# Attention with a two-layer expert tail on one core: GpSimd's first key copies and multiplications in a fixed order, block maxima and value sums moved on VectorE, weight decoding one unit later

## The chip, the core and the metric

The kernel runs on one core of one Trainium2 chip. The metric is the device time of one launch in microseconds. TensorE is PE in the rows (its weight loads are PEld), VectorE is DVE, ScalarE is ACT, GpSimd is POOL and SyncE is SP; a q behind the name (SPq, DVEq) is the sequencer of that engine.

## The reference, cut to what matters

```python
# attention: q, k, v are (2, 8, 768, 64)
k_sum = k.reshape(B, H, nb, block, D).max(axis=3)      # blocks of 32 keys: their maxima
v_sum = v.reshape(B, H, nb, block, D).mean(axis=3)     # and the means of their values
scores_l = scale * q @ k.T                             # kept where |i - j| < 16
scores_s = scale * q @ k_sum.T + log(block)
a = softmax(concat(scores_l, scores_s))                # exp, row sum, divide
x = a @ concat(v, v_sum)                               # then (1536, 512) tokens
# first layer, d_ff 2048
h = x @ moe_w_in
y = (h * sigmoid(1.702 * h)) @ moe_w_out
# second layer, d_ff 1536
out = (sigmoid(y @ moe2_w_gate) * (y @ moe2_w_val)) @ moe2_w_out
```

## The kernel before, in words

The attention is cut into 24 units, `units[u] = (b, g, hp)`: two batches b, three groups g of four query blocks of 64, four pairs of heads hp. Units 0 to 11 are of the first batch, 12 to 23 of the second. A unit goes through these steps, each a function of its own:

- `w_copy`: the keys that the four query blocks see, and the block maxima beside them, are copied and scaled into a tile `kx`, in two instructions (L698 on ScalarE for units 0 and 1, L700 on GpSimd from unit 2). The block maxima `ks` are made once for each batch and pair of heads by `prep_k` (L686, VectorE), so the second instruction of a `kx` waits for them.
- `b_pe` (L720, L722, TensorE): the scores `ps_s`. `b_max` (L728, VectorE): the row maxima `nm`. `b_exp` (L736, ScalarE): four exponentials with row sums `sm`.
- `n_inv` (L743, L745, VectorE): reciprocal `rr` of the sums. `n_mul` (L750, GpSimd): `e` times `rr`.
- `c_pe` (L756), `c_copy` (L761): transposes `ps_p` and their copy `pt`. `d_pe` (L775): values, `ps_x`. `d_hi` (L793, ScalarE) and `d_lo` (L796, VectorE): the token tile in two parts, `xH` and `xL`.

Beside the units run the value sums (`sum_v`, L668, VectorE, from the transposed values `vt`; `sum_lay`, L677 and L680, which ends in the tile `vs`: `vs_112` for the first batch, `vs_113` for the second), the decoding of weights (`load`: VectorE L132, L150 and L155, ScalarE L142 and L153; a matrix piece arrives as `raw` and leaves as `w..H` and `w..L`), and the first four of the expert layers' steps (`filler`: `first`, whose products are `ps_h` at L487, with the sigmoid at L514 and the gating at L498, L506 and L507; `second`, whose products are `ps_o` at L487).

A loop over t from -1 runs the list `ORDER` of (step, lag) at each t, step on unit t minus lag. That is only the order in which the program is written. A scheduler decides the order in which each of TensorE, VectorE, ScalarE and GpSimd gets its instructions, from its own estimate of times; at the chip each engine then works strictly in that order. Three things bind the scheduler: `in_turn` makes VectorE's attention instructions follow one another as written while t is at most `ORDERED` (4); `behind(ins, ahead["kx"])` keeps GpSimd's key copies of units 2 to 7 behind the tile that it clears at the start; and SyncE, which issues the transfers, keeps the written order. SyncE's queue is therefore one line: `vwin<-vs` of the second batch (L647) must wait for `vs_113` (L680 on ScalarE), and behind it in the queue come the keys `k` of the last pair of heads (L623, needed by unit 15), the next weights and the last queries.

Of the kernel before, what the change touches and what calls it, by code (L numbers as in the profile page):

```python
# [14 lines left out]
ALU = mybir.AluOpType  # L15
AX = mybir.AxisListType
PSUM = bass.MemoryType.PSUM
P = 128
# [11 lines left out]
def attention_moe_moe2_kernel(ctx: ExitStack, tc: tile.TileContext, ins: dict, out: bass.AP):  # L30
    nc = tc.nc
# [4 lines left out]
    B, HP, _, S = vt.shape  # L36
    H, D = 2 * HP, 64
# [5 lines left out]
    W0 = 32  # L43
    M0 = W0 + HALO
    G = 4
# [7 lines left out]
    scale = 1.0 / float(D) ** 0.5  # L53
# [55 lines left out]
    turn, ahead = [], {}  # L109

    def behind(a, b):

        tc.add_manual_dep(
            a.ins, b.ins.name,
            mybir.DependencyInfo(mybir.DependencyClass.NoSync, mybir.DependencyReason.DATA), reason="order",
        )
# [100 lines left out]
    for layer, g, i in wanted:  # L217
        w = mats[layer][i]
        last = i == len(mats[layer]) - 1
        x = w.bitcast(U32)  # L220
# [288 lines left out]
    def first(layer, g, blk, batch=False):  # L509
        w = weights[layer, g, 0]  # L510

        def sigmoid(layer, ps):
            sg = sg_slots.tile([P, TB], F32, "sg")
            nc.scalar.activation(sg, ps, AF.Sigmoid, scale=1.702 if layer == 1 else 1.0)  # L514
            return sg

        def gated(f, ps, sg):
            gate_by((layer, g, blk, f), ps, sg)

        if batch:  # L520
            held = []
            for f in range(GF):
                held.append(project(w[0], w[1], f, blk, "ps_h"))
                yield
            held = [(ps, sigmoid(layer, ps)) for ps in held]
            yield
            for f, (ps, sg) in enumerate(held):
                gated(f, ps, sg)
            yield
            return  # L530
        for f in range(GF):
            ps = project(w[0], w[1], f, blk, "ps_h")
            gated(f, ps, sigmoid(layer, ps))
            yield
# [54 lines left out]
    def pull(n):  # L589
        for _ in range(n):  # L590
            next(coming, None)

    def need(*keys):
        for key in keys:
            tries = 0
            while key not in weights:
                pull(1)
                tries += 1
                assert tries < 100, (key, w_free, w_held)

    with tc.manual_schedule(engines={mybir.EngineType.SP}), ExitStack() as es:
# [10 lines left out]
        vwin = one.tile([P, 2 * G, H * D], F32, name="vwin")  # L612
# [4 lines left out]
        qbd, vsum, kraw, kmax, kx = {}, {}, {}, {}, {}  # L617
# [8 lines left out]
        def load_q(u, eng):  # L626

            b, g, hp = units[u]
            t = qp.tile([P, G, P], F32, tag="q", name=f"q{u}")
            eng.dma_start(out=t.rearrange("p i c -> p (i c)"), in_=q[b, g, hp])  # L630
            qbd[u] = t
# [32 lines left out]
        def sum_v(b, hp):  # L664
            if hp == 0:
                vpart[b] = vp.tile([P, HP, W0], F32, tag="vm", name=f"vm{b}")
                nc.vector.memset(vpart[b], 0.0)
            in_turn(nc.vector.tensor_reduce(  # L668
                out=vpart[b][:, hp, 0:NB], in_=vtl.pop((b, hp)).rearrange("p (n t) -> p n t", t=BLK),
                axis=AX.X, op=ALU.add,  # L670
            ))

        def sum_lay(b):
            r = vpart.pop(b)
            ps = ps_a.tile([W0, H * D], F32, tag="x", name="ps_v", bufs=2)
            for hp in range(HP):
                ins = nc.tensor.matmul(ps[:, hp * P:(hp + 1) * P], lhsT=r[:, hp], rhs=ident, start=True, stop=True)  # L677
                if b == 0:
                    behind(ins, live["last"])
            nc.scalar.activation(vsum[b][0:W0], ps, AF.Copy, scale=1.0 / BLK)  # L680

        def prep_k(b, hp):
            ks = kp.tile([P, W0], F32, tag="ks", name=f"ks{b}_{hp}")
            nc.vector.memset(ks, 0.0)
            own = kraw[b, hp][:, HALO:HALO + S].rearrange("p (n t) -> p n t", t=BLK)
            in_turn(nc.vector.tensor_reduce(out=ks[:, 0:NB], in_=own, axis=AX.X, op=ALU.max))  # L686
            kmax[b, hp] = ks

        def w_copy(u):

            b, g, hp = units[u]
            t = kxp.tile([P, G, P], F32, tag="kx", name=f"kx{u}")
            r = kraw[b, hp][:, g * G * QB:g * G * QB + P - W0]
            src = bass.AP(r.tensor, r.offset, [r.ap[0], [QB, G], [1, P - W0]])
            top = kmax[b, hp].unsqueeze(1).to_broadcast([P, G, W0])
            for to, x in ((t[:, :, W0:P], src), (t[:, :, 0:W0], top)):
                if u < 2:
                    nc.scalar.activation(to, x, AF.Copy, scale=scale)  # L698
                    continue
                ins = nc.gpsimd.tensor_scalar(out=to, in0=x, scalar1=scale, scalar2=None, op0=ALU.mult)  # L700
                if u < 2 * HP:
                    behind(ins, ahead["kx"])
            kx[u] = t

        live = {}
# [1 line left out]
        def in_turn(ins):  # L707

            if now[0] <= ORDERED:
                if turn:  # L710
                    behind(ins, turn[-1])
                turn.append(ins)

        now, ORDERED = [-1], 4

        def b_pe(u):
            b, g, hp = units[u]
# [29 lines left out]

        def n_mul(u):
            e, rr = live["e", u], live.pop(("rr", u))
            nc.gpsimd.tensor_tensor(out=e, in0=e, in1=rr.unsqueeze(2).to_broadcast([P, G, P]), op=ALU.mult)  # L750

        def c_pe(u):
            e = live.pop(("e", u))
# [41 lines left out]
        def d_lo(u):  # L795
# [4 lines left out]
        NU = len(units)  # L800
        LN, LC, LD = 1, 3, 3
        ORDER = [
            (w_copy, -1), (b_pe, 0), (b_max, 0), (n_inv, LN), (n_mul, LN),
            (c_pe, LC), (c_copy, LC), (d_pe, LD), (d_hi, LD), (b_exp, 0), (d_lo, LD),
        ]

# [3 lines left out]
        for _ in range(10):  # L810
# [31 lines left out]
            out=win, in_=win, pattern=[[0, NSLOT], [1, P - W0]], compare_op=ALU.is_gt, fill=NEG,  # L842
            base=0, channel_multiplier=-1,
        )
        ins = nc.gpsimd.affine_select(
            out=win, in_=win, pattern=[[0, NSLOT], [-1, P - W0]], compare_op=ALU.is_gt, fill=NEG,
            base=2 * HALO, channel_multiplier=1,
        )
        for x in (vwin[0:W0, 0:G, :], vsum[0]):
            zero = nc.gpsimd.memset(x, 0.0)  # L850
            behind(zero, ins)
            ins = zero
# [9 lines left out]
        def filler():  # L862
            for layer, g, blk in steps[:EARLY]:
                while (blk + 1) * 2 * HP - 1 + LD > now[0]:
                    yield
                need((1, g, 0))
                yield from first(layer, g, blk, batch=True)
                need((1, g, 1))
                yield from second(layer, g, blk, False, True)

        fill = filler()
        for t in range(-1, NU + LD):
            now[0] = t

            u = t + 2
            if t < 0:
                prep_k(0, 1)
            elif HP <= u < NU and units[u][1] == 0:
                prep_k(units[u][0], units[u][2])
            for part, lag in ORDER:  # L880
                late = lag == LD and part not in (c_pe, c_copy)
                if late and t == LD + 1:
                    part(0)
                if part is w_copy and 0 < t < HP - 1:
                    continue
                if 0 <= t - lag < NU and not (late and t == LD):
                    part(t - lag)
                if part is b_max:
                    if 0 < t < HP - 1:
                        prep_k(0, t + 1)  # L890
                        w_copy(t + 1)
                    if t in (0, 1, 3, 4):
                        sum_v(0, {0: 0, 1: 1, 3: 2, 4: 3}[t])
                    if t == 4:
                        sum_lay(0)
                        nc.vector.tensor_copy(
                            vwin[0:W0, G:2 * G, :], vsum[0][0:W0].unsqueeze(1).to_broadcast([W0, G, H * D])
                        )
            if 0 <= t < NU - QUERIES:
                load_q(t + QUERIES, nc.sync)  # L900
            if t == 0:
                load_v(0, 1)
                fetch()
            if t in (5, 8):
                fetch()
            if t in (7, 8, 9, 10):
                sum_load(1, t - 7)
            if t in (8, 9, 10, 11):
                sum_v(1, t - 8)
            if t == 11:  # L910
                sum_lay(1)

            if t % HP == HP - 1 and HP < t < NU - HP:
                c = t // HP + 1
                load_v(c // NG, c % NG)
                put_v(c // NG, c % NG)
            if 8 <= t < 8 + HP:
                load_k(1, t - 8)
            if t > ORDERED:
                pull(1 if t > 9 else 2)  # L920
            for _ in range(2 if t >= 8 else 1):
                next(fill, None)
# [151 lines left out]
```

## Time and profile before

| | us |
|---|---|
| median of 3 runs (lowest, highest) | 628.85 (627.6, 629.54) |
| the profiled execution, its time | 628.51 |
| its span, first to last instruction | 626.7 |
| TensorE busy in the span | 604.9 |
| VectorE, ScalarE, GpSimd busy | 466.3, 307.1, 213.3 |
| mean granted TensorE clock, as a share of full speed | 0.992 |

A row of a timeline gives the start and the duration of an instruction (or of a few alike, with their count), its line, what it writes and reads, and in brackets how long the engine was idle before it and who ended that. Times are from the start of the span. 1.81 us of the execution's time lie outside the span.

### The profile page before, as it was taken

To read this page: it belongs to the slowest core of one execution; us is meant where nothing else is said; L and a number is where in the kernel's file an instruction comes from. 1 tells how busy PE (TensorE), PEld (TensorE's weight loads), DVE (VectorE), ACT (ScalarE), POOL (GpSimd) and SP (SyncE) were. 2 spreads that over 40 slices of the span, in tenths; PEclk is the share of its full clock that TensorE was granted. 3 is DMA by queue.
4 is the path that set the end of the run, shared out by engine and by line. 5 is a ranking of instruction groups with operands and counts; after the bars stand their busy time and mean duration, and the time that the engine had idled before them with its cause. 6 is when DMAs were issued, how large, how long until landed. Compare 5 with 4: busy or idle time off the path is not lost.

```text
span 626.7 us, 8835 instructions
## 1 busy us (share of the span) xinstructions
PE 604.9 (97%) x3360; PEld 503.0 (80%) x3360; DVE 466.3 (74%) x685; ACT 307.1 (49%) x616; POOL 213.3 (34%) x166
## 2 busy tenths in 40 slices
PE   5889979999999999999999999999999999999997
PEld 3766767778887888888888888888888888898896
DVE  6589755469898779696769979766977777877434
ACT  4489655746443345343445557653434434344230
POOL 5967864314264423241332231120220121131030
PEclk9899989999999999999999999999999999999999
DMA  9996833014221123021202003420411221100014
GB/s 312 362 325 213 250 127 67 3 47 155 68 70 65 68 67 122 13 68 67 68 1 68 0 1 135 134 68 1 134 68 44 91 68 61 75 1 1 0 41 160
DMA packets 25017, 57.83 MB, mean 92 GB/s; under 512 B 1552, under 2 KB 1808, under 8 KB 24976
## 3 DMA queue, kind: packets, MB, share of 16 engines
q1 hardware_dynamic: 24400, 56.24, 27.1%
q10 hardware_dynamic: 576, 1.05, 0.4%
q8 instruction: 26, 0.43, 0.3%
q14 instruction: 15, 0.12, 0.1%
HBM read 53.08 MB, written 3.15 MB: 90 GB/s over the span
## 4 chain that ended last, share of the span: by engine, by line
PE 79%; DMA 6%; issue 5%; ACT 4%; POOL 3%; DVE 3%; SPq 0%; ACTq 0%; POOLq 0%; DVEq 0%
PE ps_o L487 32%; PE ps_y L191 15%; PE ps_x L191 10%; PE ps_v L191 10%; PE ps_h L487 5%; PE ps_h L191 3%; DMA q<-in_q 2%; POOL gl L507 2%; DMA vt<-in_vt 2%; PE ps_s L722 2%; DMA raw<-in_moe_w_out 1%; PE ps_x L775 1%; ACT e L736 1%; PE ps_p L756 1%; DMA k<-in_k 1%
## 5 line engine op out<-in xcount | busy, mean ns | idle before, releaser
L507 POOL TENSOR_TENSOR gl<-sg,gh 128x512 fp32r<-128x512 f32 x84 | 126.1, 1507 | 368.6 <-ACT gh L506 263.1
L570 DVE TENSOR_TENSOR acc<-ps_o,acc 128x512 f32<-128x512 f32 x143 | 95.9, 684 | 46.8 <-PE ps_o L487 46.6
L487 PE MATMUL ps_o<-gl,w_1H 128*128 128x512 f32 x192 | 75.5, 394 | 1.2 <-POOL gl L507 1.2
L487 PE MATMUL ps_o<-gh,w_1L 128*128 128x512 f32 x192 | 72.2, 397 | 3.3 <-DVE sg L498 2.7
L487 PE MATMUL ps_o<-gh,w_1H 128*128 128x512 f32 x192 | 74.9, 391 | 0.0
L506 ACT CAST gh<-sg 128x512 fp32r<-128x512 f32 x84 | 51.4, 619 | 47.0 <-DVE sg L498 37.6
L487 PE MATMUL ps_o<-w_2L,gh 128*128 128x512 f32 (+1 forms) x146 | 56.6, 388 | 0.0
L487 PE MATMUL ps_o<-w_2H,gh 128*128 128x512 f32 (+1 forms) x146 | 56.2, 386 | 0.0
L487 PE MATMUL ps_o<-w_2H,gl 128*128 128x512 f32 (+1 forms) x146 | 56.2, 389 | 0.1
L150 DVE SCALAR_TENSOR_TENSOR da<-da,db 128x1024 uint32<-128x1024 uint32 x34 | 45.7, 1344 | 5.7 <-ACT da L142 5.1
L142 ACT ACTIVATE da<-da 128x1024 f32<-128x1024 f32 x34 | 36.2, 1063 | 26.1 <-DVE da L132 24.3
L487 PEld LDWEIGHTS ps_o<-gh,w_1L 128*128 128x128 f32 x192 | 35.9, 188 | 12.4 <-DVE sg L498 3.2
L487 PEld LDWEIGHTS ps_o<-gl,w_1H 128*128 128x128 f32 x192 | 36.2, 189 | 9.4 <-POOL gl L507 2.4
L487 PEld LDWEIGHTS ps_o<-gh,w_1H 128*128 128x128 f32 x192 | 36.2, 189 | 7.4
L487 PE MATMUL ps_h<-xL,w_0H 128*128 128x512 f32 x96 | 37.8, 394 | 1.8 <-DVE xL L796 1.8
L487 PE MATMUL ps_h<-xH,w_0L 128*128 128x512 f32 x96 | 37.7, 403 | 0.0
L487 PE MATMUL ps_h<-xH,w_0H 128*128 128x512 f32 x96 | 37.4, 390 | 0.0
L736 ACT ACTIVATE e<-ps_s,nm 128x128 f32<-128x128 f32 x96 | 34.4, 385 | 4.7 <-DVE nm L728 2.9
L722 PEld LDWEIGHTS ps_s<-kx,q 128*128 128x128 f32 x192 | 26.6, 206 | 9.8 <-POOL kx L700 7.3
L750 POOL TENSOR_TENSOR e<-e,rr 128x512 f32<-128x512 f32 x24 | 27.4, 1145 | 19.0 <-DVE rr L745 13.7
L722 PE MATMUL ps_s<-kx,q 128*128 128x128 f32 x192 | 27.6, 291 | 4.8 <-DMA q<-in_q 3.1
L700 POOL TENSOR_SCALAR kx<-k 128x384 f32<-128x384 f32 x22 | 29.0, 1323 | 9.0 <-DMA k<-in_k 7.8
(245 smaller groups left out, 1507.1 us busy)
## 6 DMA issues: line engine op xcount, KB each, us to landing
raw<-in_moe_w_out SPq DMA_DIRECT2D x13, 1024.0 KB, 4.8
raw<-in_moe_w_in SPq DMA_DIRECT2D x8, 1024.0 KB, 6.9
raw<-in_moe_w_gate SPq DMA_DIRECT2D x6, 1024.0 KB, 5.2
raw<-in_moe_w_val SPq DMA_DIRECT2D x6, 1024.0 KB, 5.0
q<-in_q SPq DMA_DIRECT2D x20, 256.0 KB, 8.6
vwin<-in_v SPq DMA_DIRECT2D x6, 768.0 KB, 8.0
k<-in_k SPq DMA_DIRECT2D x8, 400.0 KB, 6.5
out<-acc SPq DMA_DIRECT2D x11, 256.0 KB, 2.0
```

The source lines that it names most:

```text
L142: ins = nc.scalar.activation(af, af, AF.Prelu, scale=REBIAS, alpha=-2.0 ** 32)
L150: nc.vector.scalar_tensor_tensor(out=a, in0=a, scalar=3, in1=b, op0=ALU.logical_shift_left, op1=ALU.bitwise_or)
L191: nc.tensor.matmul(ps, lhsT=a[x][:, kk, :], rhs=b[y][:, kk, :], start=start and i == 0, stop=i == n - 1, skip_group_check=True,)
L487: nc.tensor.matmul(ps, lhsT=a, rhs=b, start=i == 0, stop=i == n - 1)
L506: nc.scalar.copy(gh, sg)
L507: nc.gpsimd.tensor_tensor(out=gl, in0=sg, in1=gh, op=ALU.subtract)
L570: nc.vector.tensor_tensor(out=a[:, m, :], in0=ps, in1=a[:, m, :], op=ALU.add)
L700: ins = nc.gpsimd.tensor_scalar(out=to, in0=x, scalar1=scale, scalar2=None, op0=ALU.mult)
L722: ins = nc.tensor.matmul(ps[:, j, :], lhsT=t[:, j, :], rhs=kt[:, j, :], start=False, stop=j == G - 1)
L736: ahead["exp"] = nc.scalar.activation(e[:, j, :], s[:, j, :], AF.Exp, bias=nm[:, j:j + 1], accum_out=sm[:, j:j + 1])
L750: nc.gpsimd.tensor_tensor(out=e, in0=e, in1=rr.unsqueeze(2).to_broadcast([P, G, P]), op=ALU.mult)
L756: nc.tensor.transpose(ps[:, j, :], e[:, j, :], ident)
```

## The change

GpSimd's chain becomes explicit: a new helper `spread` puts each of its key copies and multiplications of units 0 to 7 behind the one written before it. The written order itself is changed: within one t the row maxima come first, `w_copy` moves behind `n_inv` and runs two units ahead in place of one, and a table `between` names what is written behind which step: the block maxima of unit 3 behind the reciprocal of unit 0 (t = 1), the value sums of pairs 2 and 3 at t = 3 instead of 3 and 4, `sum_lay(0)` behind the scores of unit 4. `ORDERED` goes from 4 to 5, which also lets the decoding of weights (`if t > ORDERED: pull(...)`) begin one unit later. No instruction is added or taken away.

```diff
+        def spread(ins, u):
+
+            if u < 2 * HP:
+                behind(ins, ahead["kx"])
+                ahead["kx"] = ins
...
-                ins = nc.gpsimd.tensor_scalar(out=to, in0=x, scalar1=scale, scalar2=None, op0=ALU.mult)
-                if u < 2 * HP:
-                    behind(ins, ahead["kx"])
+                spread(nc.gpsimd.tensor_scalar(out=to, in0=x, scalar1=scale, scalar2=None, op0=ALU.mult), u)
...
-        now, ORDERED = [-1], 4
+        now, ORDERED = [-1], 5
...
-            nc.gpsimd.tensor_tensor(out=e, in0=e, in1=rr.unsqueeze(2).to_broadcast([P, G, P]), op=ALU.mult)
+            spread(nc.gpsimd.tensor_tensor(out=e, in0=e, in1=rr.unsqueeze(2).to_broadcast([P, G, P]), op=ALU.mult), u)
...
-            (w_copy, -1), (b_pe, 0), (b_max, 0), (n_inv, LN), (n_mul, LN),
+            (b_pe, 0), (b_max, 0), (n_inv, LN), (w_copy, -2), (n_mul, LN),
...
+        between = {
+            (b_max, 0): [lambda: sum_v(0, 0)],
+            (b_max, 1): [lambda: prep_k(0, 2)],
+            (n_inv, 1): [lambda: prep_k(0, 3), lambda: w_copy(2)],
+            (b_max, 2): [lambda: sum_v(0, 1)],
+            (b_max, 3): [lambda: sum_v(0, 2), lambda: sum_v(0, 3)],
+            (b_pe, 4): [lambda: sum_lay(0)],
+            (b_max, 4): [means],
+        }
...
-                if part is b_max:
-                    if 0 < t < HP - 1:
-                        prep_k(0, t + 1)
-                        w_copy(t + 1)
-                    if t in (0, 1, 3, 4):
-                        sum_v(0, {0: 0, 1: 1, 3: 2, 4: 3}[t])
-                    if t == 4:
-                        sum_lay(0)
...
+                for then in between.get((part, t), ()):
+                    then()
```

Since the scheduler works from the written order, the instructions move on every engine up to the point where unit 20 or so is reached; behind it all five engines have the same order as before. Three places follow.

GpSimd at the start, before (the tiles `kx_239`, `kx_267`, `kx_283`, `kx_315` are those of units 2, 3, 4 and 5):

```order
L700 TENSOR_SCALAR kx_239<-ks_2_236 128x4x32
L700 TENSOR_SCALAR kx_267<-k_3_154 128x4x96
L700 TENSOR_SCALAR kx_283<-k_0_138 128x4x96
L700 TENSOR_SCALAR kx_283<-ks_0_194 128x4x32
L750 TENSOR_TENSOR e<-e,rr 128x512
L700 TENSOR_SCALAR kx_315<-k_1_142 128x4x96
L700 TENSOR_SCALAR kx_315<-ks_1_197 128x4x32
L700 TENSOR_SCALAR kx_267<-ks_3_264 128x4x32
L750 TENSOR_TENSOR e<-e,rr 128x512
```

The same place in the change (`kx_246`, `kx_249`, `kx_274`, `kx_300` are those of units 2, 3, 4 and 5):

```order
L706 TENSOR_SCALAR kx_246<-ks_2_236 128x4x32
L706 TENSOR_SCALAR kx_249<-k_3_154 128x4x96
L706 TENSOR_SCALAR kx_249<-ks_3_243 128x4x32
L754 TENSOR_TENSOR e<-e,rr 128x512
L706 TENSOR_SCALAR kx_274<-k_0_138 128x4x96
L706 TENSOR_SCALAR kx_274<-ks_0_194 128x4x32
L754 TENSOR_TENSOR e<-e,rr 128x512
L706 TENSOR_SCALAR kx_300<-k_1_142 128x4x96
L706 TENSOR_SCALAR kx_300<-ks_1_197 128x4x32
```

The second half of unit 3's keys stood five instructions behind its first half, behind all of units 4 and 5; it now follows it at once, and the multiplications alternate with the copies.

ScalarE around the value sums of the second batch (`vs_113`), before (`acc_0_864` is the first layer's output of token block 0, `gh_0_0_0_808` and `gh_0_0_1_813` its gated inputs):

```order
L514 ACT_TABLE_LOAD
L514 ACTIVATE sg<-ps_h 128x512 x2
L153 CAST w_1_0H<-da 128x1024
L736 ACT_TABLE_LOAD
L736 ACTIVATE e,sm<-ps_s,nm 128x128 x3
L680 ACTIVATE vs_113<-ps_v 32x512
L736 ACTIVATE e,sm<-ps_s,nm 128x128
L793 CAST xH_777<-ps_x 128x256
L506 CAST gh_0_0_0_808<-sg 128x512
L506 CAST gh_0_0_1_813<-sg 128x512
```

The same place in the change, from the second gated input on:

```order
L506 CAST gh_0_0_1_807<-sg 128x512
L566 COPY acc_0_862<-ps_o 128x512 x2
L740 ACT_TABLE_LOAD
L740 ACTIVATE e,sm<-ps_s,nm 128x128 x4
L797 CAST xH_774<-ps_x 128x256
L566 COPY acc_0_862<-ps_o 128x512
L142 ACTIVATE da<-da 128x1024
L740 ACTIVATE e,sm<-ps_s,nm 128x128 x3
L680 ACTIVATE vs_113<-ps_v 32x512
```

`vs_113` stood inside the exponentials of unit 12, ahead of the gated inputs; it now stands inside those of unit 13, behind the gated inputs, three copies of `ps_o` and one more step of decoding.

VectorE around the decoding of `raw_2_1`, the seventh weight piece, before (the two `nm` are those of units 15 and 16):

```order
L132 TENSOR_SCALAR da<-raw_2_0_801 128x1024
L150 SCALAR_TENSOR_TENSOR da<-da,db 128x1024
L498 TENSOR_TENSOR sg<-ps_h,sg 128x512
L132 TENSOR_SCALAR db<-raw_2_1_1116 128x1024
L728 TENSOR_REDUCE nm<-ps_s 128x4 x2
L498 TENSOR_TENSOR sg<-ps_h,sg 128x512
```

The same place in the change (the two `nm` are units 15 and 16, the single one unit 17):

```order
L150 SCALAR_TENSOR_TENSOR da<-da,db 128x1024
L800 TENSOR_TENSOR xL_775<-ps_x,xH_774 128x256
L732 TENSOR_REDUCE nm<-ps_s 128x4 x2
L800 TENSOR_TENSOR xL_775<-ps_x,xH_774 128x256
L765 COPY pt<-ps_p 128x512
L747 TENSOR_SCALAR rs<-sm 128x4
L732 TENSOR_REDUCE nm<-ps_s 128x4
L749 RECIPROCAL rr<-rs 128x4
L570 TENSOR_TENSOR acc_0_862<-ps_o,acc_0_862 128x512 x2
L747 TENSOR_SCALAR rs<-sm 128x4
L749 RECIPROCAL rr<-rs 128x4
L132 TENSOR_SCALAR db<-raw_2_1_1119 128x1024
```

The first instruction that reads `raw_2_1` stood ahead of the row maxima of units 15 and 16, and stands now behind those of units 15, 16 and 17.

## Rows read from the trace of the kernel before

**Rows 1.** Windows: stretch, length, busy time by engine, granted clock, DMA share, GB/s

```profile
2.00:56.00 54.00, 44.06 (x410) 33.73 (x409) 39.72 (x83) 34.90 (x127) 41.56 (x39) 0.94 1.03 346
2.00:88.00 86.00, 69.96 (x578) 53.16 (x577) 62.50 (x120) 56.57 (x182) 64.87 (x61) 0.94 0.87 289
82.00:88.00 6.00, 3.21 (x10) 2.05 (x9) 3.97 (x8) 3.29 (x10) 3.93 (x5) 0.76 0.30 110
88.00:200.00 112.00, 110.47 (x677) 89.26 (x676) 83.56 (x123) 60.49 (x138) 46.75 (x35) 1.00 0.21 66
```

**Rows 2.** The chain of work that ended last, 29 to 88 us: start, us, what

```profile
61.91 5.20 DMA k<-in_k
...
73.20 9.27 DMA raw<-in_moe_w_out
...
96.79 0.89 PE ps_s L722 x8
...
98.29 0.59 PE ps_p L756 x4
```

**Rows 3.** Timeline of GpSimd, 9 to 84 us

```profile
12.34 2.30 POOL L700 TENSOR_SCALAR kx<-k 128x384 f32<-128x384 f32 x2 [0.97 <-DMA k<-in_k]
...
17.24 1.02 POOL L700 TENSOR_SCALAR kx<-ks 128x128 f32<-128x128 f32 x2
...
28.89 2.14 POOL L700 TENSOR_SCALAR kx<-k 128x384 f32<-128x384 f32 x1
...
71.94 1.33 POOL L700 TENSOR_SCALAR kx<-ks 128x128 f32<-128x128 f32 x2
```

**Rows 4.** Timeline of VectorE, 9 to 84 us

```profile
21.67 0.69 DVE L728 TENSOR_REDUCE nm<-ps_s 128x4 f32<-128x512 f32 x1 [6.79 <-PE ps_s L722]
...
28.27 1.72 DVE L896 COPY vwin<-vs 32x2048 f32<-32x2048 f32 x1
...
40.19 0.95 DVE L668 TENSOR_REDUCE vm<-vt 128x24 f32<-128x768 f32 x1 [1.89 <-DMA vt<-in_vt]
...
48.13 0.95 DVE L668 TENSOR_REDUCE vm<-vt 128x24 f32<-128x768 f32 x1 [0.82 <-DMA vt<-in_vt]
...
52.10 0.41 DVE L796 TENSOR_TENSOR xL<-ps_x,xH 128x256 fp32r<-128x256 f32 x1
...
82.56 0.73 DVE L132 TENSOR_SCALAR db<-raw 128x1024 uint32<-128x1024 uint32 x1 [2.95 <-DMA raw<-in_moe_w_out]
83.22 1.27 DVE L728 TENSOR_REDUCE nm<-ps_s 128x4 f32<-128x512 f32 x2
```

**Rows 5.** Timeline of ScalarE, 53 to 66 us

```profile
56.24 1.08 ACT L514 ACTIVATE sg<-ps_h 128x512 f32<-128x512 f32 x2
...
59.57 0.37 ACT L736 ACTIVATE e<-ps_s,nm 128x128 f32<-128x128 f32 x1
...
60.61 0.57 ACT L680 ACTIVATE vs<-ps_v 32x512 f32<-32x512 f32 x1
```

**Rows 6.** VectorE by line and shape, 8 to 100 us: busy us, mean ns, idle before

```profile
L150 DVE SCALAR_TENSOR_TENSOR da<-da,db 128x1024 uint32<-128x1024 uint32 x5 | 6.6, 1318 | 1.2 <-ACT da L142 1.2
...
L132 DVE TENSOR_SCALAR db<-raw 128x1024 uint32<-128x1024 uint32 x5 | 4.3, 851 | 3.0 <-DMA raw<-in_moe_w_out 3.0
...
L498 DVE TENSOR_TENSOR sg<-ps_h,sg 128x512 f32<-128x512 f32 x4 | 2.7, 679 | 0.7 <-ACT sg L514 0.7
...
L155 DVE TENSOR_TENSOR w_0L<-da,w_0H 128x1024 fp32r<-128x1024 f32 x2 | 2.4, 1196 | 0.0
```

**Rows 7.** What the queue of SyncE waited for, 0 to 90 us: total, times, longest

```profile
SPq L647 <- ACT xH L793: 9.9, 1, 9.9
```

**Rows 8.** Timeline of SyncE's queue, 28 to 90 us: start, us, issue

```profile
62.54 0.78 SPq L231 DMA_DIRECT2D raw<-in_moe_w_in  x1
```

**Rows 9.** DMA issues, 55 to 90 us: count, KB each, median us to landing

```profile
raw<-in_moe_w_in SPq DMA_DIRECT2D x2, 1024.0 KB, 8.2
```

**Rows 10.** Timeline of TensorE, 98 to 99.5 us

```profile
98.63 0.48 PE L487 MATMUL ps_h<-xH,w_0L 128*128 128x512 f32 x1
```

More of the change, by code (lines that the diff above doesn't have):

```diff
@@ L869, in filler, with means @@
                 yield from second(layer, g, blk, False, True)
+        def means():
+            nc.vector.tensor_copy(
+                vwin[0:W0, G:2 * G, :], vsum[0][0:W0].unsqueeze(1).to_broadcast([W0, G, H * D])
+            )
+        between = {
[7 more added lines that the diff above has]
+        }
         fill = filler()
@@ L877, in attention_moe_moe2_kernel @@
                 prep_k(0, 1)
+                w_copy(0)
             elif HP <= u < NU and units[u][1] == 0:
@@ L883, in attention_moe_moe2_kernel @@
                     part(0)
-                if part is w_copy and 0 < t < HP - 1:
+                if part is w_copy and t == 0:
                     continue
@@ L887, in attention_moe_moe2_kernel @@
                     part(t - lag)
-                if part is b_max:
-                    if 0 < t < HP - 1:
-                        prep_k(0, t + 1)
-                        w_copy(t + 1)
-                    if t in (0, 1, 3, 4):
-                        sum_v(0, {0: 0, 1: 1, 3: 2, 4: 3}[t])
-                    if t == 4:
-                        sum_lay(0)
-                        nc.vector.tensor_copy(
-                            vwin[0:W0, G:2 * G, :], vsum[0][0:W0].unsqueeze(1).to_broadcast([W0, G, H * D])
-                        )
+                for then in between.get((part, t), ()):
+                    then()
             if 0 <= t < NU - QUERIES:
```

## The prediction

> **What bounds the kernel now.** I read the windows first. From 88 us on TensorE is full: 110.47 of 112 us. From 2 to 88 it works 69.96 of 86, so 16.0 us are idle [rows 1]. The change reorders nothing behind unit 20 or so, which lies near 100 us; hence it can give at most those 16.0, and whatever it gives must show as an earlier time at which TensorE reaches a fixed place in its order. I take the first `ps_h` of token block 1, at 98.63 [rows 10], as that place.
>
> The transfers come next. Their share is 1.03 from 2 to 56 us [rows 1]: the transfer engines are full there, so what lands in that stretch lands when it did, whoever asks earlier. After it SyncE's queue stands for 9.9 us at L647 [rows 7]: the queue waits for `vs_113`, which ScalarE ends at 60.61 + 0.57 = 61.18 [rows 5], and only then are `k` of the last pair of heads (issued 61.91, landed 67.11) and `raw_2_0` (issued 62.54) sent [rows 2, 8].
>
> The timelines give three waits of VectorE [rows 4]. At the start it idles 6.79 us until 21.67, for scores of unit 3, whose second half of keys GpSimd makes only at 17.24 + 0.5 = 17.7 [rows 3]. At 40.19 and 48.13 it waits 1.89 and 0.82 us for `vt` tiles. At 82.56 it has waited 2.95 us for `raw_2_1` (issued 73.20, 9.27 us [rows 2]), while the row maxima of units 15 and 16, queued behind, come at 83.22. In 82 to 88 TensorE works 3.21 of 6 us at a granted clock of 0.76 [rows 1], a mean between the two levels, 1.2 and 2.4 GHz; it had been idle just before. That is the hole which the chain passes through.
>
> **The start (spread, block maxima of unit 3).** GpSimd's work from 12.34 on is the same, in another order. `kx` of unit 3 is complete after its second half, 0.5 behind the pair that takes 12.34 to 14.6 in the old order [rows 3]; with the half directly behind the first it is there at about 13.5 to 14. Scores take 0.89 [rows 2], so the row maximum of unit 3 can stand at 15 instead of 21.67. That is not 6.7 us of gain: GpSimd is then the slower of the two, and units 4 to 7 still need all of its copies. Ahead of the first `vt` of the second batch the new order has two row maxima, one L132, one L150 and two `xL` more than the old one: 1.4 + 0.85 + 1.32 + 0.8 = 4.4 us [rows 4, 6], 3.7 when the 0.08 are taken off by which successive rows overlap. VectorE, 6 us early at the start, has the time for them and reaches the wait that much further on. The wait itself stays at 40.2, since the transfer is not sooner (at most by 0.5 us, from gaps in the full stretch).
>
> **From 40.2 to the first sigmoids.** What is left for VectorE between that landing and the `xL` of unit 7 are, in the new order, one block sum (0.95), two L132 steps (0.85 each), one row maximum (0.69), one L155 (1.20) and two `xL` (0.41 each): 5.4 us [rows 4, 6]. So `xL` is at 45.6 to 45.7 where it was at 52.10; before, the second `vt` wait and more decoding stood ahead of it. The first sigmoids followed it by 4.1 us (52.10 to 56.24 [rows 4, 5]); the new queue of ScalarE has less ahead of them, about 2.1, so 47.8 instead of 56.24. This is the gain of the change for TensorE, since the first layer's products come some 8 us sooner and fill what is idle between 46 and 70.
>
> **The value sums come later.** From the second wait (48.13, unchanged) the new order has 22 VectorE instructions up to the row maximum of unit 13: three reductions of `vt` and three of `k` (0.95 each), one L150 (1.32), two L132 (0.85), one L155 (1.20), two gatings and two `pt` of the same size (0.68), two row maxima (0.69), three `xL` (0.41), three small ones (0.2) [rows 4, 6]: 5.7 + 1.3 + 1.7 + 1.2 + 2.7 + 1.4 + 1.2 + 0.6 = 15.8. Successive rows overlap by about 0.08, 1.7 in all, and I add 0.7 for waits on ScalarE: the maximum ends at 62.9. `vs_113` stands behind three exponentials: in the old order 1.04 from the first of them to `vs_113`, and 0.57 for itself [rows 5]. With a hand-over this gives 64.8 instead of 61.18: **3.6 us later**, and with it `k` (67.11 to 70.7) and `raw_2_0` (issued 66.1). The latter landed by 62.54 + 8.2 = 70.7 [rows 8, 9]; now 74.3.
>
> **Unit 15.** Behind the landing GpSimd finished `kx` of unit 15 at 71.94 + 1.33 = 73.27, 6.2 after `k` [rows 2, 3]; now 76.9, and its scores are done at 77.8. VectorE has, from 70.7: a block maximum (0.95), `xL`, gating, `pt`, gating (0.41 + 3 x 0.68), then L132 twice from `raw_2_0` at 74.3 (1.7), `pt` (0.68), L150 (1.32), `xL` (0.41): 78.4, and with hand-overs 78.9 for the row maximum of unit 15, instead of 83.22, because `raw_2_1` (which would land near 85) is no longer ahead of it. Three sets of exponentials (some 1.4 each, four of 0.34 [rows 5]) lead to 83.1, and two additions, `raw_2_1`'s step, an `xL` and another addition, 3.5 us with their hand-overs, to the last inputs of the fixed place at about 87; its place in TensorE's order decides. There TensorE has 62 matmuls between unit 15's scores and the first `ps_h` of block 1. At the mean of the full stretch, 110.47 / 677 = 0.163 us [rows 1], these take 10.1: 77.8 + 10.1 = 87.9. I take **88.0 instead of 98.63**, 10.6 sooner. In the old order the scores of unit 20 (0.89) and the transposes of unit 15 (0.59 [rows 2]) are already done there, in the new one they come behind: 1.5 less, 9.1. Some 25 hand-overs that I listed nowhere, at 0.05, cost 1.2: a gain of 7.9.
>
> **The sum.** The profiled execution took 628.51, its span and 1.81 around it, 0.34 below the median of the three runs: 628.5 - 7.9 = **620.6**. Bounds: if all of TensorE's idle time went, 612.5; if only the later value sums count, 628.5 + 3.6 = 632.1. The clock's dip probably moves ahead of the scores of unit 15 (70 to 78) instead of vanishing, which is in neither count; in 82 to 88 the dip cost 0.24 x 3.21 = 0.8 us.
>
> **A rule weighed.** GpSimd's copy at 28.89 took 2.14 where an undisturbed one takes 1.15 (2.30 for two); VectorE's copy ran from 28.27 to 29.99 beside it, so of 1.10 us in common 0.99 was lost [rows 3, 4]. The Trainium skill, "SBUF — State Buffer", section "SBUF: two separate sides", says that the two engines share a port pair as an exclusive lock, and that a VectorE instruction in a two-port mode or with two SBUF inputs makes the other block for the whole instruction. By that rule the trace agrees here, and it speaks against moving decoding beside GpSimd's gating; the sum by it is that of the first rival.
>
> **Rivals.**
> First, collisions: with the sigmoids 8 us sooner, GpSimd's gating and copies of units 12 to 14 fall beside VectorE's decoding (L132, L150, L155) at 48 to 62. For it speaks the copy at 28.89; against it, that such collisions exist before too. Two more full losses of 0.97 ahead of `vs_113` make `k` 1.9 later: 622.5.
> Second, larger gain: `vs_113` is not later, because VectorE does not wait at 48.13 or ScalarE is ahead. Then 3.6 comes back: 617.0. Against it, the full transfer engines.
> Third, nothing is gained: the new order says other things but the landings at 40 and 48 hold everything, and what unit 15 gains from `raw_2_1` goes to the later `k`. No gain: 628.5.
> Fourth, slower: the start's advance is used up by GpSimd's equal work before 40 us, the first sigmoids stay near 56, and `k` still comes 3.6 later, with all of TensorE's queue from unit 15's scores on: 632.1. It decides at 3.6 us: with sigmoids no sooner than 52.6 nothing is gained, later than that the kernel loses. My 47.8 is 4.8 us from it.
>
> **How the numbers follow.** The forecast, 617 to 624.5, has 0.55; collisions 0.10; the larger gain 0.08; no gain 0.13; slower 0.14. A difference of 0.3% (1.9 us) is about what can be told here, so below 626.9 is faster: 0.55 + 0.10 + 0.08 = 0.73; same 0.13; slower 0.14. The range 615.5 to 629.5 leaves out the slower case, about half of the larger gain and a little of no gain, 0.2 together.
>
> **What the new profile would show.** Right: a row maximum of unit 3 near 15 with no wait of 6.8 behind it; waits for `vt` still near 40 and 48; first sigmoids near 48; `vs_113` ending near 65 and `k` landing near 71; no wait for `raw_2_1` ahead of unit 15's maxima, which come near 79; TensorE full in 82 to 88 and its hole at 70 to 78; the first `ps_h` of block 1 near 88. Wrong: `vt` waits that move with the start (transfers not bound), sigmoids after 52.6, a wait for `raw_2_0` ahead of unit 15 that ends after 78, or idle TensorE behind 88, where I count on it being full.

## The result and the profile after

The changed kernel takes **621.06 us** (median of 3 runs, 621.02 to 622.46) where the kernel before took 628.85: a ratio of 0.9886, 95% interval 0.9854 to 0.9919. 620.6 us was forecast. The profiled execution took 621.02 us with a span of 619.2, 7.5 us shorter than the span before.

TensorE first, by windows of the changed kernel (same columns as [rows 1]):

```profile
2.00:88.00 86.00, 75.95 (x654) 59.01 (x653) 67.67 (x129) 59.57 (x201) 66.11 (x63) 0.94 0.89 286
8.00:12.00 4.00, 2.06 (x14) 1.41 (x13) 2.90 (x5) 2.90 (x16) 1.67 (x2) 0.95 1.05 380
12.00:17.00 5.00, 4.20 (x19) 3.84 (x19) 3.75 (x7) 1.53 (x9) 4.71 (x6) 0.50 1.04 318
...
70.00:76.00 6.00, 4.79 (x37) 3.49 (x35) 3.51 (x9) 3.39 (x5) 4.30 (x5) 1.00 0.91 331
76.00:82.00 6.00, 5.40 (x52) 4.72 (x49) 6.00 (x9) 3.09 (x6) 6.00 (x6) 1.00 0.74 198
82.00:88.00 6.00, 5.47 (x41) 4.22 (x40) 3.23 (x10) 4.45 (x25) 6.00 (x8) 1.00 1.03 334
88.00:200.00 112.00, 110.48 (x633) 89.28 (x633) 87.51 (x123) 58.64 (x122) 47.90 (x34) 1.00 0.24 74
```

Up to 88 us it has done 654 instructions in 75.95 us, where [rows 1] had 578 in 69.96. Behind 88 us it is as full as before (110.48 against 110.47 of 112). In 82 to 88 it works 5.47 us at full clock instead of 3.21 at 0.76. So the time was won ahead of 88 us and nothing was given back.

GpSimd's timeline of the changed kernel (start, us):

```profile
12.29 1.17 POOL L706 TENSOR_SCALAR kx<-k 128x384 f32<-128x384 f32 x1 [1.03 <-DMA k<-in_k]
13.43 0.53 POOL L706 TENSOR_SCALAR kx<-ks 128x128 f32<-128x128 f32 x1
...
64.80 1.04 POOL L754 TENSOR_TENSOR e<-e,rr 128x512 f32<-128x512 f32 x1 [2.46 <-DVE rr L749]
```

VectorE's, which answers to [rows 4]:

```profile
16.12 0.69 DVE L732 TENSOR_REDUCE nm<-ps_s 128x4 f32<-128x512 f32 x1 [0.92 <-PE ps_s L726]
...
40.52 0.95 DVE L668 TENSOR_REDUCE vm<-vt 128x24 f32<-128x768 f32 x1
...
45.67 0.39 DVE L800 TENSOR_TENSOR xL<-ps_x,xH 128x256 fp32r<-128x256 f32 x1
49.25 0.95 DVE L668 TENSOR_REDUCE vm<-vt 128x24 f32<-128x768 f32 x1 [3.19 <-DMA vt<-in_vt]
...
56.99 2.09 DVE L155 TENSOR_TENSOR w_0L<-da,w_0H 128x1024 fp32r<-128x1024 f32 x1
...
64.96 1.96 DVE L150 SCALAR_TENSOR_TENSOR da<-da,db 128x1024 uint32<-128x1024 uint32 x1 [0.34 <-ACT da L142]
...
71.54 0.95 DVE L686 TENSOR_REDUCE ks<-k 128x24 f32<-128x768 f32 x1 [1.29 <-DMA k<-in_k]
...
75.97 0.70 DVE L132 TENSOR_SCALAR da<-raw 128x1024 f32<-128x1024 f32 x1 [0.61 <-DMA raw<-in_moe_w_in]
...
79.85 1.27 DVE L732 TENSOR_REDUCE nm<-ps_s 128x4 f32<-128x512 f32 x2
...
87.46 0.96 DVE L132 TENSOR_SCALAR db<-raw 128x1024 uint32<-128x1024 uint32 x1 [1.07 <-DMA raw<-in_moe_w_out]
```

ScalarE's, for [rows 5]:

```profile
49.60 1.08 ACT L514 ACTIVATE sg<-ps_h 128x512 f32<-128x512 f32 x2
...
65.81 0.57 ACT L680 ACTIVATE vs<-ps_v 32x512 f32<-32x512 f32 x1
```

What SyncE's queue waited for, for [rows 7], and TensorE's timeline, for [rows 10]:

```profile
SPq L647 <- ACT e L740: 14.7, 1, 14.7
```

```profile
89.76 0.47 PE L487 MATMUL ps_h<-xH,w_0L 128*128 128x512 f32 x1
```

The reader is to see four things. The second half of unit 3's keys is made at 13.43, and the row maximum of unit 3 comes at 16.12 instead of 21.67, with a wait of 0.92 instead of 6.79. VectorE reaches the first `vt` almost as it lands, and has done more by then: its wait has moved to the second one (3.19 instead of 0.82). `vs_113` comes 5.2 us later than before, and SyncE's queue stands 14.7 us for it instead of 9.9. And unit 15's row maxima still come 3.4 us sooner (79.85 against 83.22), with `raw_2_1` behind them.

### The profile page after: what moved, and what is told of

Read it like the earlier page. It is cut to its first block, busy times and chain, and to the rows that moved or that the text cites. A ratio compares the mean times of both kernels' runs of the same rounds, so it can differ in the third digit from the quotient of the medians.

```text
span 619.2 us, 8841 instructions
## 1 busy us (share of the span) xinstructions
PE 603.3 (97%) x3360; PEld 502.7 (81%) x3360; DVE 468.0 (76%) x685; ACT 306.0 (49%) x616; POOL 213.1 (34%) x166
## 3 DMA queue, kind: packets, MB, share of 16 engines
q1 hardware_dynamic: 24400, 56.24, 27.8%
## 4 chain that ended last, share of the span: by engine, by line
PE 77%; DMA 9%; issue 5%; ACT 3%; POOL 3%; DVE 2%; SPq 0%; ACTq 0%; POOLq 0%; DVEq 0%
PE ps_o L487 32%; PE ps_y L191 15%; PE ps_x L191 10%; PE ps_v L191 10%; PE ps_h L487 4%; PE ps_h L191 4%; DMA raw<-in_moe_w_in 3%; DMA q<-in_q 2%; DMA vt<-in_vt 2%; POOL gl L507 2%; DMA vwin<-in_v 1%; ACT e L740 1%; PE ps_s L726 1%; PE ps_x L779 1%; PE ps_p L760 1%
## 5 line engine op out<-in xcount | busy, mean ns | idle before, releaser
L507 POOL TENSOR_TENSOR gl<-sg,gh 128x512 fp32r<-128x512 f32 x84 | 127.4, 1523 | 362.9 <-ACT gh L506 261.0
L150 DVE SCALAR_TENSOR_TENSOR da<-da,db 128x1024 uint32<-128x1024 uint32 x34 | 46.7, 1373 | 4.9 <-ACT da L142 4.3
L754 POOL TENSOR_TENSOR e<-e,rr 128x512 f32<-128x512 f32 x24 | 28.8, 1204 | 15.2 <-DVE rr L749 9.8
L487 PEld LDWEIGHTS ps_o<-w_2H,gh 128*128 128x128 f32 x146 | 27.4, 188 | 5.7
```

Source lines behind the costliest of these rows:

```text
L150: nc.vector.scalar_tensor_tensor(out=a, in0=a, scalar=3, in1=b, op0=ALU.logical_shift_left, op1=ALU.bitwise_or)
L487: nc.tensor.matmul(ps, lhsT=a, rhs=b, start=i == 0, stop=i == n - 1)
L507: nc.gpsimd.tensor_tensor(out=gl, in0=sg, in1=gh, op=ALU.subtract)
L754: spread(nc.gpsimd.tensor_tensor(out=e, in0=e, in1=rr.unsqueeze(2).to_broadcast([P, G, P]), op=ALU.mult), u)
```

## The experiments

Each kernel was compared with the kernel before on the same chip. Times are medians, ratios have their 95% interval.

**GpSimd's chain alone** (kernel before):

```diff
+        def spread(ins, u):
+            if u < 2 * HP:
+                behind(ins, ahead["kx"])
+                ahead["kx"] = ins
...
-                ins = nc.gpsimd.tensor_scalar(out=to, in0=x, ...)
-                if u < 2 * HP:
-                    behind(ins, ahead["kx"])
+                spread(nc.gpsimd.tensor_scalar(out=to, in0=x, ...), u)
...
-            nc.gpsimd.tensor_tensor(out=e, in0=e, ...)
+            spread(nc.gpsimd.tensor_tensor(out=e, in0=e, ...), u)
```

> The kernel before with GpSimd's chain alone: copies and multiplications of units 0 to 7 one behind the other in the old written order, decoding as before. Theory A (the start decides: unit 3's keys come early, VectorE is ahead at the first vt wait, the first layer's sigmoids come sooner, and raw_2_1 stands behind unit 15's maxima): most of the change's gain is here, 621 to 624 us, the row maximum of unit 3 at 16 to 17 us without the wait of 6.8 us, first sigmoids before 52 us. Rival B (decoding one unit later is what counts): 627 to 630 us. Rival C (the written order counts, block maxima and value sums sooner): at most 2 us of gain, 626 to 629 us.

Measured: 621.87 us, 0.9885 (0.9867 to 0.9903). The chain alone gives the whole gain; rivals B and C fall. Its timelines of VectorE and ScalarE have one row each that theory A did not expect together with this time:

```profile
17.30 0.69 DVE L732 TENSOR_REDUCE nm<-ps_s 128x4 f32<-128x512 f32 x1 [1.81 <-PE ps_s L726]
```

```profile
55.25 1.08 ACT L514 ACTIVATE sg<-ps_h 128x512 f32<-128x512 f32 x2
```

The start is early, but the first sigmoids come only 1.0 us sooner than before (56.24 [rows 5]), and the gain is there all the same. In this order too `raw_2_1` (first read at 91.00) stands behind the maxima of units 15 to 17, so the chain brings both that place and the early start.

**The change without the chain:**

```diff
-                ahead["kx"] = ins
...
-            spread(nc.gpsimd.tensor_tensor(out=e, in0=e, ...), u)
+            nc.gpsimd.tensor_tensor(out=e, in0=e, ...)
```

> The changed kernel without GpSimd's chain: the copies of units 2 to 7 only behind the tile that is cleared, as before; written order and decoding as changed. Here the second half of unit 3's keys stands three instructions behind the first. Theory A: part of VectorE's wait at the start is back (2 to 4 us) and vs_113 and k are as late as in the change, so 623 to 628 us. Rival B and rival C: the gain stays, 620 to 622 us.

Measured: 629.58 us, 1.0014 (1.0002 to 1.0026): nothing is left, and theory A, with 623 to 628 us, had lost less. VectorE's timeline, and TensorE's window from 34 to 46 us (same columns as above):

```profile
20.25 0.69 DVE L731 TENSOR_REDUCE nm<-ps_s 128x4 f32<-128x512 f32 x1 [5.70 <-PE ps_s L725]
...
40.22 0.95 DVE L668 TENSOR_REDUCE vm<-vt 128x24 f32<-128x768 f32 x1 [6.08 <-DMA vt<-in_vt]
```

```profile
34.00:46.00 12.00, 6.76 (x63) 5.92 (x62) 5.92 (x12) 6.75 (x27) 3.58 (x4) 0.73 1.05 284
```

5.70 of the 6.79 us at the start are back, and then VectorE stands 6.08 us at the first `vt`, with work queued behind it that it could have done; TensorE works 6.76 of 12 us there. In this order `raw_2_1` too stands behind the maxima of units 15 to 17, so that place brings no gain where VectorE stands like this ahead of it.

**Decoding one unit sooner in the change, and one unit later in the kernel before:**

```diff
-        now, ORDERED = [-1], 5
+        now, ORDERED = [-1], 4
```

> The changed kernel with decoding a unit sooner again (ORDERED 4). Theory A: the start is as in the change, the row maximum of unit 3 near 16 us, 619 to 623 us; the first sigmoids may even come sooner. Rival B: the gain is gone, 626 to 630 us.

Measured: 620.64 us, 0.9868 (0.9851 to 0.9885): as the change.

```diff
-        now, ORDERED = [-1], 4
+        now, ORDERED = [-1], 5
```

> The kernel before with decoding one unit later (ORDERED 5) and nothing else. In this order raw_2_1 stands behind the maxima of units 15 and 16 but ahead of unit 17's. Theory A: the wait of 6.8 us at the start stays, the first sigmoids stay after 54 us, and only what raw_2_1 held comes back: 624.5 to 628.5 us. Rival B: the whole gain, 620 to 622 us.

Measured: 627.25 us, 0.9969 (0.9952 to 0.9986). Decoding later is worth about 2 us in the kernel before (0.9 to 3.0 by the interval), and beside the chain nothing that could be measured.

**`raw_2_1` behind unit 17's maximum** (kernel before, in `load`, with the maxima kept in `ahead["nm", u]`):

```diff
+            elif (layer, g, i) == (1, 2, 1):
+                behind(ins, ahead["nm", 17])
```

> The kernel before with one order alone: VectorE's first step on raw_2_1 behind the row maximum of unit 17. Nothing else is bound, so the start's wait of 6.8 us stays. Theory A: row maxima of unit 15 at 78 to 80 us instead of 83.2 and the hole at 82 to 88 us mostly closed, 625 to 627.5 us, that is less than half of the change's gain. Rival F (the wait for raw_2_1 was the whole cost): 620 to 622 us. Rival G (the hole opens elsewhere): 628 to 630 us.

Measured: 624.96 us, 0.9932 (0.9915 to 0.9949). VectorE's timeline:

```profile
21.78 0.69 DVE L730 TENSOR_REDUCE nm<-ps_s 128x4 f32<-128x512 f32 x1 [7.20 <-PE ps_s L724]
...
79.76 1.29 DVE L730 TENSOR_REDUCE nm<-ps_s 128x4 f32<-128x512 f32 x2 [0.25 <-PE ps_s L724]
```

With the start untouched and unit 15 at 79.76, 3.9 us are won: half of the change's gain; the time lies just under theory A's range. So in the kernel before that wait did cost what it delayed (83.22 - 79.76 = 3.5 us). This is the cleanest of the experiments: in its trace TensorE, ScalarE and GpSimd have the same order as in the kernel before, and VectorE's alone differs.

**The keys of the last pair of heads ahead of the `vwin` transfers,** in the change and in the kernel before:

```diff
+            if 8 <= t < 8 + HP:
+                load_k(1, t - 8)
             if t % HP == HP - 1 and HP < t < NU - HP:
                 c = t // HP + 1
                 load_v(c // NG, c % NG)
                 put_v(c // NG, c % NG)
-            if 8 <= t < 8 + HP:
-                load_k(1, t - 8)
```

> The changed kernel with the keys of the last pair of heads written ahead of the two vwin transfers in SyncE's queue, so that they no longer wait for vs_113. Theory A (unit 15 is paced by the late keys, and TensorE's holes in 70 to 88 us come from that): k lands before 62 us, row maxima of unit 15 before 77 us, 617.5 to 620 us. Rival D (TensorE has other work while it waits, the late keys cost nothing): 620.5 to 622 us.

Measured in the change: 620.89 us, 0.9878 (0.985 to 0.9907), as without it. VectorE's timeline:

```profile
65.53 1.23 DVE L150 SCALAR_TENSOR_TENSOR da<-da,db 128x1024 uint32<-128x1024 uint32 x1 [0.34 <-ACT da L142]
...
73.61 0.69 DVE L732 TENSOR_REDUCE nm<-ps_s 128x4 f32<-128x512 f32 x1 [0.64 <-PE ps_s L726]
```

The row maximum of unit 15 came at 73.61, 6.2 us sooner than in the change, and the time did not move by more than the runs scatter. By its number rival D holds: in the change TensorE has other work while it waits for unit 15. The scheduler had a part in this: with the keys moved it placed TensorE's instructions anew, and at 136 of 3360 places they differ from those of the change.

> The kernel before with the keys of the last pair of heads written ahead of the two vwin transfers. In this order raw_2_1 stands behind the maxima of units 15 and 16. Theory A: k lands before 62 us and the hole at 82 to 88 us closes, but VectorE's wait of 6.8 us at the start stays: 624 to 627 us. Rival D: 628 to 630 us.

Measured in the kernel before: 624.87 us, 0.9935 (0.9912 to 0.9958). There the same edit is worth 4.0 us, as theory A had it. But these are not the keys' alone: TensorE's order differs from that of the kernel before at 277 places, and on VectorE the first step on `raw_2_1` (81.40) stands behind the maxima of units 15 and 16 (76.27), and the place behind units 15 to 17 won 3.9 us by itself (above). What the keys add was not taken apart.

**The fifth weight piece ahead as well** (the edit above, and the two `vwin` transfers written at t = 13 behind `pull`):

```diff
-            if t % HP == HP - 1 and HP < t < NU - HP:
+            if t in (7, 15, 19):
...
+            if t == 13:
+                load_v(1, 0)
+                put_v(1, 0)
```

> The changed kernel with both the keys of the last pair of heads and the fifth weight piece (raw_2_0) ahead of the two vwin transfers in SyncE's queue. Theory A: neither unit 15's keys nor raw_2_0 waits for vs_113, so VectorE does not wait for raw_2_0 and 70 to 82 us fills: 616.5 to 619.5 us, not slower than with the keys alone. Rival D: 620.5 to 622 us. Rival E (the value windows are now sent later and unit 12's ps_x waits for them): 621 to 625 us.

Measured: 621.55 us, 0.9879 (0.9857 to 0.9901). Nothing more. The number lies in the ranges of both rival D and rival E; but TensorE shows no wait for `vwin` ahead of a `ps_x` before 90 us, which speaks for D. Theory A's condition was not met either: queries stood ahead in the queue, `raw_2_0` was issued at 64.82, and VectorE still waited 1.03 us for it, until 70.45 (75.97 in the change).

**Unit 4's copies behind unit 3's second half, and nothing else** (kernel before):

```diff
+                if u == 3:
+                    ahead["kx3"] = ins
+                elif u == 4:
+                    behind(ins, ahead["kx3"])
```

> The kernel before with one constraint alone: GpSimd's copies of unit 4 behind the second half of unit 3's keys. The multiplications stay where the scheduler puts them, decoding as before; in this order raw_2_1 stands behind the maxima of units 15 to 17. Theory A (unit 3's keys and the place of raw_2_1 make the gain): the row maximum of unit 3 at 16 to 18 us, 621 to 624.5 us. Rival H (the alternation of multiplications and copies matters too): 625 to 628 us, with VectorE waiting for GpSimd's e or keys between 17 and 40 us.

Measured: 626.8 us, 0.9969 (0.9955 to 0.9983): theory A missed, and rival H's range holds. VectorE's timeline:

```profile
18.20 0.69 DVE L732 TENSOR_REDUCE nm<-ps_s 128x4 f32<-128x512 f32 x1 [2.84 <-PE ps_s L726]
...
30.95 0.20 DVE L747 TENSOR_SCALAR rs<-sm 128x4 f32<-128x4 f32 x1 [2.33 <-ACT e L740]
...
74.08 1.29 DVE L732 TENSOR_REDUCE nm<-ps_s 128x4 f32<-128x512 f32 x2
```

Unit 3 is early and unit 15 too (74.08), and still only 2.3 us are won. The multiplications stand elsewhere than in the chain, but the sign of rival H is not there as it was described: at 30.95 VectorE waits for ScalarE. Part of what is missing is lost later. Behind 88 us TensorE is busy for 108.17 of 112 us, 2.3 less than before and in the change, and two of its waits there are for gated inputs from ScalarE:

```profile
108.88 0.74 PE L487 MATMUL ps_o<-gh,w_1L 128*128 128x512 f32 x2 [1.15 <-ACT gh L506]
...
112.48 0.50 PE L487 MATMUL ps_o<-gh,w_1L 128*128 128x512 f32 x1 [1.05 <-ACT gh L506]
```

The rest, some 3 us, was not taken apart, nor which order makes these waits.

**The row maximum of unit 15 behind `raw_2_1` in the change** (in `load`, for the first step on `raw_2_1`, with the maxima kept in `ahead["nm", u]`):

```diff
+            elif (layer, g, i) == (1, 2, 1) and x["out"] is b:
+                behind(ahead["nm", 15], ins)
```

> The changed kernel with one order turned back: the row maximum of unit 15 behind VectorE's first step on raw_2_1, as it was before the change. raw_2_1 landed at 87.4 us in the changed kernel, so the maximum of unit 15 comes at about 88 instead of 79.9 us. Theory A' (revised: the place of raw_2_1 is worth about as much as the whole change, because the later value sums make raw_2_1 later too): 626 to 631 us, a hole in TensorE at 82 to 92 us. Rival I (the earlier start alone is the gain): 621 to 624 us.

Measured: 623.33 us, 0.9918 (0.9901 to 0.9935). Its VectorE, and its TensorE behind 88 us:

```profile
16.16 0.69 DVE L734 TENSOR_REDUCE nm<-ps_s 128x4 f32<-128x512 f32 x1 [0.46 <-PE ps_s L728]
...
87.39 0.70 DVE L132 TENSOR_SCALAR db<-raw 128x1024 uint32<-128x1024 uint32 x1 [1.13 <-DMA raw<-in_moe_w_out]
88.00 1.28 DVE L734 TENSOR_REDUCE nm<-ps_s 128x4 f32<-128x512 f32 x2
```

```profile
88.00:94.00 6.00, 5.00 (x29) 3.85 (x28) 3.56 (x9) 5.23 (x24) 1.04 (x1) 1.00 0.09 35
```

Unit 15 came 8.1 us later than in the change, as expected, but that cost 2.3 us at most against the median on record, and 1.2 against the change on the same chip. Theory A' falls, and by its number rival I holds: without the place of `raw_2_1` 5.8 us are left. But more than one order was turned back. The scheduler answered the edit: TensorE's order differs from the change's at 56 places, and the products of block 1 begin at 86.72, ahead of unit 15's transposes, where the change has them at 89.76:

```profile
86.72 0.39 PE L489 MATMUL ps_h<-xH,w_0L 128*128 128x512 f32 x1
```

So TensorE has no hole in 82 to 88 (6.00 of 6 us) and pays behind it (5.00 of 6 in 88 to 94). What the delay costs with TensorE's order as in the change, no run shows.

**Early decoding and the early keys together** (both edits above, on the change):

> The changed kernel with decoding one unit sooner (ORDERED 4) and the keys of the last pair of heads ahead of the two vwin transfers. The two together had 620.6 and 620.9 us alone. Theory A: TensorE's idle time between 52 and 82 us shrinks a little more, 618 to 620.5 us. Rival D (what is left is bound by transfers before 56 us and by the start): 620 to 621.5 us, no more than either alone.

Measured: 621.05 us, 0.9877 (0.9863 to 0.9892): no version tried beats the change by more than the runs scatter.

**The change once more,** on the chip of the last three:

> The changed kernel itself, on the chip of the three others, for comparing with them: 620.5 to 622 us.

Measured: 622.13 us, 0.9887 (0.987 to 0.9904), 0.1 over the range expected.

## Why the prediction was right, and where it was not

The median lies 0.5 us above the forecast and the gain is 7.8 us where 7.9 was worked out. Not all steps under that sum held.

**The start: right.** 15 was forecast for unit 3's row maximum, 16.12 came; the `xL` of unit 7 stood at 45.67, as forecast. The chain alone gives the gain, and without it nothing is left: that is shown from both sides. How the chain comes to its gain is a question apart, and the early start is only a part of the answer (below).

**First sigmoids: mis-sized, and not what I took them for.** 47.8 was forecast, 49.60 came, 6.6 us sooner than before: the `xL` ahead of them stood at its place, but they followed it by 3.9 us where 2.1 was counted. The step that called this "the gain of the change for TensorE" failed. The chain alone has its sigmoids at 55.25 and the same time; and since its `vs_113` ends at 63.56, 2.4 us later than before, the fourth rival's rule (no gain unless the sigmoids come sooner by what `vs_113` comes later) would have made it slower. It is refuted.

Nor did TensorE fill up between 46 and 70: in the change it was busy for 21.56 us there at a clock of 0.93, before for 21.86 at 0.97. These are its windows (same columns as [rows 1]), of the kernel before:

```profile
2.00:46.00 44.00, 34.06 (x320) 26.37 (x319) 30.54 (x67) 27.24 (x103) 34.05 (x33) 0.94 1.03 345
46.00:58.00 12.00, 12.00 (x105) 8.74 (x105) 11.18 (x21) 9.66 (x28) 8.98 (x9) 0.93 0.92 308
58.00:82.00 24.00, 20.69 (x148) 16.00 (x147) 16.81 (x26) 16.38 (x43) 17.91 (x17) 1.00 0.71 221
```

of the change:

```profile
2.00:46.00 44.00, 38.73 (x374) 30.47 (x373) 35.38 (x76) 30.47 (x118) 35.84 (x34) 0.92 1.05 337
46.00:58.00 12.00, 9.56 (x71) 6.80 (x70) 8.70 (x14) 7.54 (x17) 8.75 (x8) 0.86 0.97 334
58.00:82.00 24.00, 22.18 (x173) 17.51 (x172) 20.36 (x32) 17.10 (x44) 15.51 (x15) 1.00 0.52 157
```

and of the chain alone:

```profile
2.00:46.00 44.00, 35.28 (x345) 26.56 (x344) 33.44 (x70) 29.31 (x112) 33.83 (x33) 0.96 1.05 335
46.00:58.00 12.00, 9.47 (x90) 6.49 (x88) 9.95 (x19) 8.16 (x21) 8.21 (x8) 1.00 0.96 331
58.00:82.00 24.00, 23.39 (x157) 19.18 (x157) 19.64 (x31) 18.96 (x49) 18.53 (x18) 0.93 0.42 131
82.00:88.00 6.00, 6.00 (x51) 4.93 (x50) 4.78 (x10) 3.97 (x22) 6.00 (x8) 1.00 1.04 288
```

Busy time multiplied by the granted clock is an estimate of the work done, in us at full clock. By it the change leads the kernel before by 3.6 us at 46, by only 0.7 at 58 (VectorE has stood 3.19 us for the second `vt`), by 2.2 at 82 and by 5.2 at 88: 3.0 of that come in 82 to 88, where the kernel before had its hole. The chain alone leads by 1.9, 0.2, 1.2 and 4.8, the second execution of the change by 5.4, 1.8, 2.7 and 4.0. So in all three what the start wins by 46 us is for the most part gone at 58, and a third to three quarters of the lead at 88 comes from the last 6 us, by the closing of the hole that the forecast named. The early start alone does not carry the gain.

The work done by 88 us goes with the time, though not alone. The row "2.00:88.00" of each trace has it, here as instructions and as that estimate (one product for the whole row, so up to 0.5 off the sum above), and beside it TensorE's busy time in the row "88.00:200.00":

| kernel | profiled time | TensorE instructions, 2 to 88 us | busy x clock, us | busy, 88 to 200 us |
|---|---|---|---|---|
| change without the chain | 628.69 | 611 | 64.3 | 108.58 |
| before | 628.51 | 578 | 65.8 | 110.47 |
| before, decoding later | 628.43 | 595 | 63.5 | 111.05 |
| unit 3 and 4 alone | 627.33 | 626 | 67.4 | 108.17 |
| before, early keys | 624.87 | 625 | 68.3 | 110.15 |
| `raw_2_1` behind | 624.86 | 618 | 67.7 | 110.47 |
| change once more | 623.90 | 638 | 70.1 | 110.49 |
| change, `raw_2_1` ahead | 622.85 | 653 | 72.2 | 108.26 |
| change, early keys and fifth piece | 622.82 | 664 | 70.6 | 108.59 |
| chain alone | 622.06 | 639 | 71.2 | 110.82 |
| change, early decoding and keys | 621.05 | 641 | 71.1 | 111.04 |
| change | 621.02 | 654 | 71.4 | 110.48 |
| change, early decoding | 620.99 | 651 | 72.8 | 110.53 |
| change, early keys | 619.79 | 652 | 73.7 | 110.47 |

Two executions of the change itself differ by 1.3 us in the fourth column, so differences of that size in it say nothing. In four kernels TensorE is busy for 1.9 to 2.3 us less behind 88 us than in the kernel before. That fits the one with `raw_2_1` ahead, which is third by the fourth column and yet not among the fastest; so what is lost behind 88 counts too. The two columns together do not rank every kernel either: the change without the chain is behind the kernel before in both and only 0.2 us slower.

**The later value sums: mis-sized.** `vs_113` ended at 66.38 instead of the 64.8 forecast. Two terms were short: the second `vt` landed at 49.25, not 48.13, and one L155 (at 56.99) took 2.09 us where 1.20 was counted, beside GpSimd.

**What they cost: wrong.** The forecast of unit 15's path (79.85 came for 78.9, 89.76 for 88.0 at the first `ps_h` of block 1, 8.9 us sooner and not 10.6) treated it as what sets the end. In the kernel before it was: `raw_2_1` behind, with TensorE's order untouched, won 3.9 us. In the changed order it is nearly free: keys early enough to bring unit 15's maximum to 73.61 won 0.2 us, and 8.1 us of delay cost about 1 to 2. (In both of these the scheduler had placed TensorE's instructions anew, so what they show is the price once the order has been made for it.) So the second rival's "3.6 comes back" and the fourth's 632.1 did not exist in this form.

That the sum came out so close is partly luck. 8.9 less the 1.5 of work done out of order is 7.4, against 7.5 of the span; that step is sound, and the second execution bears it out (first `ps_h` at 92.69, 5.9 sooner, less 1.5 is 4.4; its span is 4.6 shorter). But the mark came 1.8 us later than forecast, and the 1.2 for hand-overs behind it, which no run shows, happened to stand in for that.

**The clock: misplaced.** The dip was expected at 70 to 78; there the clock was 1.00. It lay at 12 to 17 (0.50) and, a mean of 0.86, at 46 to 58. Over 2 to 88 us it was 0.94 in both kernels, so in these two executions the clock does not set them apart.

**Collisions: the first rival's mechanism is there, its price is not.** VectorE's L150 at 64.96 began 0.16 us behind GpSimd's multiplication of 64.80 and took 1.96 us, while the multiplication took its 1.04. With the early keys the two began in the other order:

```profile
65.70 1.95 POOL L754 TENSOR_TENSOR e<-e,rr 128x512 f32<-128x512 f32 x1
```

That is GpSimd's timeline of that kernel; VectorE's L150 had begun at 65.53 and took 1.23. So the one that is second loses 0.73 to 0.91 us, and the first nothing. The Trainium skill, "SBUF — State Buffer", section "SBUF: two separate sides", says that whichever of the two starts first holds the shared port pair for its whole instruction and the other blocks; by that rule the trace agrees, here in both directions. Ahead of `vs_113` the rival had two more losses of 0.97; one of 0.89 (L155) was there. That the losses fell on a path with time to spare is argued from the price of unit 15's path above; no run takes the collisions away.

**Left open.** Which of the orders that follow from the chain keeps the hole at 82 to 88 closed and TensorE full behind it, where the constraint on units 3 and 4 alone keeps only 2.3 us of the gain; whether a start earlier still would be paid, since GpSimd is busy without a gap in 17 to 40 us and the transfers are full until 56.

## What to carry to other kernels

Order the engine that paces the start by hand when a scheduler decides by its own estimates: here one chain of GpSimd's instructions was worth the whole change, and the rewritten order around it nothing that could be measured. Price a late step by trying it both ways, sooner and later, in the kernel that is to be judged: the wait for `raw_2_1` was worth 3.9 us before the change and 1 to 2 behind it. When a constraint is put in to test one order, compare the orders of all engines in the two traces first: of the edits on unit 15's path only `raw_2_1` behind unit 17's maximum left the other engines as they were. And ask in which stretch the bottleneck gained: a lead at 46 us can be gone at 58. A mark such as the first `ps_h` of a block is a poor clock between kernels whose orders differ: in the kernel before with early keys it came 1.0 us later (99.62) and the profiled time was 3.6 us shorter. The work done by a fixed time ranks them better, if what is lost behind that time is looked at too.

## What the runs showed of the hardware

TensorE's granted clock was 0.50 in 12 to 17 us of the change, the lower of its two levels (1.2 of 2.4 GHz), after a stretch in which it had worked 2.06 of 4 us; so the earlier scores of units 2 and 3 ran at half speed, which no term of the forecast had. In the second profile of the same kernel TensorE had worked 1.75 of 4 us in 8 to 12, and the clock did not fall:

```profile
12.00:17.00 5.00, 2.79 (x21) 2.17 (x20) 3.71 (x6) 2.41 (x12) 4.32 (x6) 1.00 1.05 307
```

Over 2 to 88 us it was 0.98 there instead of 0.94. So this dip does not come in every execution; what decides it stays open.
